# Softmax sums of a batch gathered in one PSUM bank by 128x32 column tiles and spread by DMA

## The chip, the cores and the metric

The kernel runs on one core of a Trainium2 chip. The metric is the device time of one execution in microseconds (us), the median over several executions.

## What is computed

Two layers, for a batch of 8, with 8 heads, 1024 positions and head size 64. The inputs are float32, the kernel computes in bf16 with float32 sums.

```
k_proj = einsum('ks,bhsd->bhkd', E, k)          # 1024 positions -> 64
v_proj = einsum('ks,bhsd->bhkd', F, v)
p      = exp(q @ k_proj^T / 8)                  # 64 scores per position
attn   = p / sum(p)                             # the softmax sums
x      = attn @ v_proj                          # -> (8192, 512), heads side by side
h      = max(x @ w1, x @ w2, x @ w3)            # 512 -> 768
out    = h @ w_out                              # 768 -> 512
```

## The kernel before, in words

**Stages.** Batch b is one sample of 1024 positions. The second layer of batch b is the frame of the program. It is done in two chunks (`ch` 0 and 1) of 512 positions. Each chunk has ten steps, named here (ch, step): steps 0 to 5 are `up` (L550), one for each 128 of the 768 hidden columns, with 12 matmuls of 128x512 (three weight matrices, four contraction tiles); steps 6 to 9 are `down` (L596), one for each 128 positions, with 6 matmuls of 128x512. So a batch has 144 and 48 such matmuls.

**The maximum of an up step.** Its three products lie in three PSUM banks. ScalarE copies the first to `h1s` (L566), VectorE takes the maximum of the second with it (`m12`, L570) and of the third with that (`hT`, L518). `down` needs all six `hT` pieces, the last one in its sixth matmul.

**Attention is slipped in between.** `plan(b)` (L626) is a list written by hand: after step (ch, step) of batch b, do these pieces for the next batch n = b+1 (or n+1). The pieces work on a pair g of heads, four pairs in a batch:

- `kproj`, `vproj` (L340, L365): 16 matmuls each of 128x256, in tiles of 128 rows by 64 columns of TensorE; then copies `kp`, `vp` by VectorE and ScalarE. `kt` transposes `kp` (two matmuls, L353).
- `sc` (`scores`, L195): four 64x64 tiles, 512 columns each, called a pass here; ScalarE's exponential `pT` (L213) is deferred to a `run_later` behind the next `h1s` copy.
- `za`: one pass with a matrix of ones gives the sums, already repeated over the 64 rows of a head (`sums`, L229); one pass gives the values times `vp` (`values`, L244, both L222); ScalarE turns the sums into reciprocals in a logarithm `zl` (L235) and an exponential `zi` (L241) of 128x1024; VectorE multiplies values and `zi` into `xT` (`scale_x`, L252).
- `qd` (L321): VectorE packs q in four copies (`q_p`), and one DMA transpose on SP's queue makes `qT` (L333).
- `ld` (L188): loads q, k and v of a later batch, three DMAs on POOL's queue (L191). The load of q waits for the DMA transpose of the batch before it.

**What sets the order.** Each engine runs its instructions in the order in which the program records them (`manual_schedule`). PSUM banks are dealt at build time: `bank()` and `two()` take the bank, or even-odd pair, that a small planner clock holds to come free first. A matmul waits on the chip until its bank's last reader is done. The stores of `out` (L619), E and F, and the DMA transposes share SP's queue; three `o_sb` buffers of two position tiles stand between `down` and the stores.

Batch 0 has an order of its own, and batch 1 and 2 have lists of their own; batches 3 to 6 use the last list of `plan`. The last batch, 7, has nothing slipped in.

Of the kernel before, what the change touches and what calls it, by code (L numbers as in the profile page):

```python
# [8 lines left out]
FP32 = mybir.dt.float32  # L9
BF16 = mybir.dt.bfloat16  # L10
AF = mybir.ActivationFunctionType
# [4 lines left out]
def kernel(  # L16
# [13 lines left out]
    nc = tc.nc  # L30
# [19 lines left out]
    const = ctx.enter_context(tc.tile_pool(name="const", bufs=1))  # L50
    loads = ctx.enter_context(tc.tile_pool(name="loads", bufs=1))
    att = ctx.enter_context(tc.tile_pool(name="att", bufs=2))
    psum = ctx.enter_context(tc.tile_pool(name="psum", bufs=1, space=bass.MemoryType.PSUM))

    ET = mybir.EngineType
# [23 lines left out]
    def bank():  # L79
        n = min(range(8), key=lambda n: free[n])  # L80
        deal((n,))
        return psum_t[:, n, :], (n,)

    def pe(dt, wait=0.0):
        clock["pe"] = max(clock["pe"], wait) + dt
        return clock["pe"]

    def runs(eng, ready, dt, ns=()):
        if eng in clock:
            clock[eng] = max(clock[eng], ready + 0.06) + dt  # L90
            for n in ns:
                free[n] = clock[eng]
            return clock[eng]
        return ready + dt
# [22 lines left out]

    ident = const.tile([P, P], BF16, name="ident")
    ones = const.tile([P, HALF], BF16, name="ones")
    warm = const.tile([P, 512], BF16, name="warm")  # L120
    warm_f = const.tile([P, 512], FP32, name="warm_f")
    w_sb = [const.tile([P, NCT, DF], BF16, name=f"w{i}_sb") for i in range(3)]
# [49 lines left out]
    nc.vector.memset(warm, 0.0)  # L172
    make_identity(nc, ident)
    nc.vector.memset(ones, 1.0)

    load_w(0, slice(0, 2))
    load_kv(2, V2)
# [31 lines left out]

    def exps(b, g, lo, nsi, sc):  # L210
        t, ns, ready = sc
        pTs[b, g, lo] = att.tile([P, 2, CHUNK], BF16, name="pT", bufs=4)[:, :, 0:nsi * HALF]
        nc.scalar.activation(out=pTs[b, g, lo], in_=t, func=AF.Exp, scale=scale)  # L213
        runs("s", ready, 0.17 + nsi * 0.107, ns)

# [13 lines left out]
    def sums(b, g, lo, nsi):  # L229
        return pair_mm(b, g, lo, nsi, lambda rows, hp: ones[rows])  # L230

    def invert(b, g, lo, nsi, z):
        t, ns, ready = z
        zl = att.tile([P, 2, CHUNK], FP32, name="zl", bufs=1)[:, :, 0:nsi * HALF]
        nc.scalar.activation(out=zl, in_=t, func=AF.Ln)  # L235
        runs("s", ready, 0.17 + nsi * 0.107, ns)
        if nsi == SI:
            zi = att.tile([P, 2, CHUNK], FP32, name="zi", bufs=2)
        else:
            zi = att.tile([P, 2, CHUNK // 2], FP32, name="zi0", bufs=4)  # L240
        nc.scalar.activation(out=zi, in_=zl, func=AF.Exp, scale=-1.0)  # L241
        zis[b, g, lo] = zi, runs("s", ready, 0.17 + nsi * 0.107)

    def values(b, g, lo, nsi):  # L244
        if b not in xTs:
            xTs[b] = att.tile([P, NCT, SI, P], BF16, name="xT")
        return pair_mm(b, g, lo, nsi, lambda rows, hp: vps[b][rows, 2 * g + hp, :])

    def scale_x(b, g, lo, nsi, av):
        t, ns, ready = av  # L250
        zi, when = zis.pop((b, g, lo))
        nc.vector.tensor_tensor(  # L252
            out=xTs[b][:, g, lo:lo + nsi, :].rearrange("a (c s) p -> a c (s p)", c=2),
            in0=t, in1=zi, op=ALU.mult,
        )
        runs("v", max(ready, when), 0.17 + nsi * 0.13, ns)
# [5 lines left out]
            f()  # L262
        later.clear()

    def sc(b, g, lo=0, nsi=SI):
        def f():
            t = scores(b, g, lo, nsi)
            later.append(lambda: exps(b, g, lo, nsi, t))
        return f

    def za(b, g, lo=0, nsi=SI, then=False):
        def f():
            z = sums(b, g, lo, nsi)
            av = values(b, g, lo, nsi)
            invert(b, g, lo, nsi, z)
            if then:
                later.append(lambda: scale_x(b, g, lo, nsi, av))
            else:
                scale_x(b, g, lo, nsi, av)
        return f  # L280
# [40 lines left out]
    def qd(b, parts=1):  # L321

        def f():
            q_p = att.tile([P, NPAIR, SI, 2, D], BF16, name="q_p", bufs=1)
            qTs[b] = att.tile([P, NPAIR * SI, P], BF16, name="qT")
            n = NPAIR // parts
            for lo in range(0, NPAIR, n):
                for g in range(lo, lo + n):
                    copy(
                        "v", q_p[:, g].rearrange("p si h d -> p h si d"),  # L330
                        qkv[b][0][:, 2 * g:2 * g + 2], (), 0.43,
                    )
                last_T[b] = nc.sync.dma_start_transpose(  # L333
                    out=qTs[b][:, lo * SI:(lo + n) * SI, :],
                    in_=q_p[:, lo:lo + n].rearrange("p g si h d -> p (g si h d)"),
                )
        return f

    kps = {}
    def kproj(b):  # L340
        def f():
            t, ns = bank()
            proj(b, 1, t, (LO, HI), 4 * D)
            kps[b] = att.tile([P, 2, 2 * D], BF16, name="kp")
            copy("v", kps[b].rearrange("a g x -> a (g x)"), t[:, 0:4 * D], ns, 0.43)
        return f

    def kt(b):
        def f():
            t, ns = two()  # L350
            t = t.bitcast(BF16)[:, 0]
            for gg in range(2):
                nc.tensor.transpose(  # L353
                    out=t[:, gg * P:(gg + 1) * P], in_=kps[b][:, gg, :], identity=ident
                )
            pe(0.2)

            kpTs[b] = att.tile([P, NPAIR, KP], BF16, name="kpT")
            copy(
                "v", kpTs[b].rearrange("a (y x) k -> a x y k", x=2),  # L360
                t[:, 0:2 * P].rearrange("a (x y k) -> a x y k", x=2, y=2), ns, 0.3,
            )
        return f

    def vproj(b):  # L365
        def f():
            t, ns = bank()
            proj(b, 2, t, (LO, HI), 4 * D)

            vps[b] = att.tile([P, H, D], BF16, name="vp")  # L370
            for hh, hs in enumerate((LO, HI)):
                i = t[hh * HALF:(hh + 1) * HALF, 0:4 * D].rearrange("a (h d) -> a h d", d=D)
                for to in range(2):
                    copy("sv"[hh], vps[b][to * HALF:(to + 1) * HALF, hs, :], i, ns, 0.4)
        return f
# [247 lines left out]
    def ld(b):  # L623
        return lambda: load(b)

    def plan(b):  # L626
        n = b + 1
        if b == 0:
            c1 = (SPC, SPC)
            return {  # L630
                (0, 6): [za(0, 1, *c1), sc(0, 3, *c1)],
                (0, 7): [qd(1, 2), za(0, 2, *c1)],
                (0, 8): [za(0, 3, *c1)],
                (1, 0): [kproj(1)],
                (1, 1): [kt(1)],
                (1, 2): [vproj(1), ld(2)],
                (1, (3, "mid")): [sc(1, 0), sc(1, 1)],
                (1, 4): [za(1, 0), sc(1, 2)],
                (1, 5): [za(1, 1), sc(1, 3)],
                (1, 7): [za(1, 2)],  # L640
                (1, 8): [za(1, 3)],
            }
        if b == 1:
            return {
                (0, 1): [qd(2)],
                (0, 5): [kproj(2), vproj(2), ld(3)],
                (0, 6): [kt(2)],
                (0, 7): [sc(2, 0)],
                (0, 9): [za(2, 0), sc(2, 1)],
                (1, 1): [za(2, 1), sc(2, 2)],  # L650
                (1, 3): [za(2, 2), sc(2, 3)],
                (1, 5): [za(2, 3)],
                (1, 6): [qd(3)],
            }
        if b == 2:
            return {
                (0, 2): [kproj(3), vproj(3), ld(4)],
                (0, 3): [kt(3)],
                (0, 4): [sc(3, 0)],
                (0, 6): [za(3, 0), sc(3, 1)],  # L660
                (1, 0): [za(3, 1), sc(3, 2), qd(4)],
                (1, 2): [za(3, 2), sc(3, 3), kproj(4), vproj(4), ld(5)],
                (1, 4): [kt(4)],
                (1, 5): [za(3, 3), sc(4, 0)],
            }
        if n == B:
            return {}
        out = {
            (0, 1): [za(n, 0), sc(n, 1)],
            (0, 3): [za(n, 1), sc(n, 2)],  # L670
            (0, 9): [za(n, 2), sc(n, 3)],
            (1, 3): [za(n, 3)],
        }
        if n + 1 < B:
            out[0, 6] = [qd(n + 1)]
            out[0, 9] += [kproj(n + 1), vproj(n + 1)]
            out[1, 1] = [kt(n + 1)]
            out[1, 3] += [sc(n + 1, 0)]
        if n + 2 < B:
            out[1, 1] += [ld(n + 2)]  # L680
        return out

    for b in range(B):
# [59 lines left out]
```

The softmax here doesn't subtract the row's maximum and nothing guards it: scores larger than these inputs give would overflow.

## Time and profile before

| | |
|---|---|
| median of 8 executions | 405.63 us (405.34 to 406.21) |
| the profiled execution | 405.7 us, of which its span is 403.7 |
| TensorE matmuls (PE) busy | 391.2 us, 97% of the span |
| VectorE (DVE) / ScalarE (ACT) busy | 203.2 us (50%) / 189.4 us (47%) |
| granted TensorE clock | 1.00 in every stretch |
| batch 2, from the start of its first up step to that of batch 3 | 122.6 to 172.9 us |
| batch 3 / 4 / 5 | 47.2 / 47.0 / 47.0 us |
| batch 6 / 7 to the end | 44.7 / 44.9 us |
| DMA moved | 53.33 MB, 132 GB/s on average |

Times in the profile are us from the span's start. A group line names the source line, the engine, the operation, output<-input, shape and count; then the busy time, the mean ns of one instruction, and the idle time in front with what ended it. Matmuls are pipelined, so a matmul of 376 ns can start every 216 ns: lengths of TensorE work are read from start to start. A few matmul records are missing, so a group may show 23 where there are 24.

### The profile page before, as it was taken

Reading aid. Unit: us, or ns where it says so; the run is one execution under the profiler, and the core shown is the slowest. Engines: PE = TensorE matmul, PEld = TensorE weight load, DVE = VectorE, ACT = ScalarE, POOL = GpSimd, SP = SyncE. Lnnn points to the kernel's source line nnn. Section 1 sums busy time; section 2 is a strip of 40 time slices with the busy share of each in tenths; the row PEclk is TensorE's granted clock in tenths of the full one; section 3 lists DMA queues with packets and bytes.
Section 4 is the critical chain, followed back from the end, with each engine's and each line's share of the span. In section 5 each row is a group of like instructions: output and inputs, shape, how many; then the busy total and the mean of one; then the engine's idle time right before and its main releaser. Section 6 shows DMA issues by size and latency. Waiting matters only on the chain.

```text
span 403.7 us, 5831 instructions
## 1 busy us (share of the span) xinstructions
PE 391.2 (97%) x2309; PEld 178.5 (44%) x2351; DVE 203.2 (50%) x314; ACT 189.4 (47%) x274; POOL 31.4 (8%) x44
## 2 busy tenths in 40 slices
PE   7899989999999999999999999999999999999996
PEld 3444443444444435444544445444544444444443
DVE  2348745761764527537353655626364363525251
ACT  2622437525672376555643555437535555432322
POOL 7430001001000100200100002000000000000000
PEclk9999999999999999999999999999999999999999
DMA  9999999959907996892799029960510202020202
GB/s 156 207 206 207 231 194 161 242 124 179 232 2 213 191 222 106 130 239 49 210 179 205 33 15 235 202 176 0 144 66 2 104 2 104 0 106 0 106 0 105
DMA packets 62667, 53.33 MB, mean 132 GB/s; under 512 B 30128, under 2 KB 58288, under 8 KB 62640
## 3 DMA queue, kind: packets, MB, share of 16 engines
q0 software_dynamic: 28512, 28.31, 44.3%
q1 hardware_dynamic: 33984, 24.51, 20.7%
q8 instruction: 18, 0.29, 0.3%
q10 hardware_dynamic: 144, 0.13, 0.1%
q14 instruction: 9, 0.07, 0.1%
HBM read 57.15 MB, written 16.78 MB: 183 GB/s over the span
## 4 chain that ended last, share of the span: by engine, by line
PE 83%; DMA 10%; ACT 3%; DVE 2%; issue 1%; POOL 0%; DVEq 0%; ACTq 0%; POOLq 0%
PE banks L508 55%; PE banks L605 18%; DMA v_t<-in_v_dram 8%; PE banks L222 4%; PE banks L286 3%; DMA k_t<-in_k_dram 2%; PE banks L202 2%; DVE xT L252 1%; ACT zl L235 1%; ACT zi L241 1%; PE banks L411 1%; ACT pT L213 0%; PE banks L437 0%; PE banks L382 0%; DVE m L570 0%
## 5 line engine op out<-in xcount | busy, mean ns | idle before, releaser
L508 PE MATMUL banks<-xT,w_sb 128*128 128x512 bf16 x1120 | 255.1, 379 | 2.7 <-issue 1.0
L508 PEld LDWEIGHTS <-w_sb 128*128 128x128 bf16 x1152 | 109.5, 98 | 137.1 <-issue 11.0
L570 DVE TENSOR_TENSOR m<-banks,h1s 128x512 f32<-128x512 f32 x90 | 62.0, 689 | 85.0 <-ACT h1s L566 52.1
L566 ACT COPY h1s<-banks 128x512 f32<-128x512 f32 x90 | 52.5, 583 | 90.3 <-PE banks L508 88.2
L605 PE MATMUL banks<-wout_sb,hT 128*128 128x512 bf16 x369 | 84.6, 379 | 1.0 <-issue 0.6
L252 DVE TENSOR_TENSOR xT<-banks,zi 128x1024 bf16<-128x1024 f32 (+1 forms) x36 | 39.8, 1106 | 73.6 <-ACT zi L241 54.2
L518 DVE TENSOR_TENSOR hT<-banks,m 128x512 bf16<-128x512 f32 x90 | 62.3, 692 | 10.0 <-PE banks L508 0.8
L99 ACT COPY o_sb<-banks 128x512 f32<-128x512 f32 (+1 forms) x56 | 32.6, 581 | 52.4 <-PE banks L605 52.4
L605 PEld LDWEIGHTS <-hT 128*128 128x128 bf16 x378 | 35.9, 98 | 45.5 <-issue 3.1
L235 ACT ACTIVATE zl<-banks 128x1024 f32<-128x1024 f32 (+1 forms) x36 | 33.5, 930 | 31.4 <-PE banks L222 30.5
L213 ACT ACTIVATE pT<-banks 128x1024 bf16<-128x1024 f32 (+1 forms) x36 | 33.2, 930 | 14.9 <-PE banks L202 14.9
L241 ACT ACTIVATE zi<-zl 128x1024 f32<-128x1024 f32 (+1 forms) x36 | 34.6, 962 | 1.1
L191 POOL DMA_DIRECT2D q_t<-in_q_dram x7 | 6.1, 877 | 203.3 <-DVE kp L99 79.8
L222 PE MATMUL banks<-pT,ones 64*64 64x512 bf16 (+1 forms) x144 | 13.7, 374 | 0.9 <-ACT pT L213 0.6
L222 PE MATMUL banks<-pT,vp 64*64 64x512 bf16 (+1 forms) x144 | 13.3, 355 | 0.4 <-DVE vp L99 0.4
L202 PE MATMUL banks<-qT,kpT 64*64 64x512 bf16 (+1 forms) x144 | 13.3, 358 | 0.3 <-DVE m L570 0.3
L286 PEld LDWEIGHTS <-efT 128*64 128x64 bf16 x224 | 11.6, 110 | 4.3 <-issue 2.7
L99 DVE CAST vp<-banks 64x256 bf16<-64x256 f32 (+1 forms) x18 | 7.1, 397 | 7.9 <-ACT vp L99 4.7
L222 PEld LDWEIGHTS <-ones 64*64 64x64 bf16 x144 | 4.4, 103 | 14.3 <-issue 14.2
L99 DVE COPY q_p<-q_t 128x1024 bf16<-128x1024 bf16 x28 | 10.0, 419 | 0.0
L99 ACT CAST vp<-banks 64x256 bf16<-64x256 f32 x14 | 5.1, 365 | 9.8 <-PE banks L286 9.6
L286 PE MATMUL banks<-v_t,efT 128*64 128x256 bf16 x112 | 7.3, 273 | 1.1 <-DMA v_t<-in_v_dram 1.1
(51 smaller groups left out, 103.9 us busy)
## 6 DMA issues: line engine op xcount, KB each, us to landing
out_dram<-o_sb SPq DMA_DIRECT2D x30, 512.0 KB, 3.3
q_t<-in_q_dram POOLq DMA_DIRECT2D x7, 1024.0 KB, 9.8
k_t<-in_k_dram POOLq DMA_DIRECT2D x7, 1024.0 KB, 14.2
v_t<-in_v_dram POOLq DMA_DIRECT2D x7, 1024.0 KB, 18.9
w_sb<-in_moe_w_dram POOLq DMA_DIRECT2D x5, 384.0 KB, 11.7
k_t<-in_k_dram POOLq DMA_DIRECT2D x2, 512.0 KB, 8.7
v_t<-in_v_dram POOLq DMA_DIRECT2D x4, 256.0 KB, 11.9
wout_sb<-in_moe_w_out_dram POOLq DMA_DIRECT2D x1, 768.0 KB, 16.1
```

Source lines behind the costliest of these rows:

```text
L99: done = {"v": nc.vector.tensor_copy, "s": nc.scalar.copy, "g": nc.gpsimd.tensor_copy}[eng](out=o, in_=i)
L213: nc.scalar.activation(out=pTs[b, g, lo], in_=t, func=AF.Exp, scale=scale)
L222: nc.tensor.matmul(out=t[hp * HALF:(hp + 1) * HALF, c, 0:nsi * HALF], lhsT=w(rows, hp), rhs=p[rows, hp, :], start=True, stop=True,)
L235: nc.scalar.activation(out=zl, in_=t, func=AF.Ln)
L241: nc.scalar.activation(out=zi, in_=zl, func=AF.Exp, scale=-1.0)
L252: nc.vector.tensor_tensor(out=xTs[b][:, g, lo:lo + nsi, :].rearrange("a (c s) p -> a c (s p)", c=2), in0=t, in1=zi, op=ALU.mult,)
L286: nc.tensor.matmul(out=t[hh * HALF:(hh + 1) * HALF, 0:width], lhsT=efT[:, si, (kv - 1) * KP:kv * KP], rhs=qkv[b][kv][:, heads[hh], si, :], ...
L508: nc.tensor.matmul(out=h, lhsT=w_sb[i][:, ct, jt * P:(jt + 1) * P], rhs=xTs[b][:, ct, ch * SPC:(ch + 1) * SPC, :], start=(ct == first), st ...
L518: nc.vector.tensor_tensor(out=o, in0=h, in1=other, op=ALU.max)
L566: nc.scalar.copy(out=h1s, in_=h[0][0])
L570: nc.vector.tensor_tensor(out=m12, in0=h[1][0], in1=h1s, op=ALU.max)
L605: nc.tensor.matmul(out=o_ps, lhsT=hTs[b, ch][:, jt, tt * P:(tt + 1) * P], rhs=wout_sb[:, jt, :], start=(jt == 0), stop=(jt == NJT - 1),)
```

## The change

From batch 3 on (prepared during batch 2), the sums of all four pairs are made together. `zc` runs 8 matmuls of 128x512 with a selecting weight `pick` of 128x32: pair g has the 32-column tile g, and the two halves of `pT` (`hp` 0 and 1) are added there by two matmuls. All results lie in one PSUM bank, each sum repeated over 8 rows. ScalarE makes the reciprocals in two instructions of 128x512. SP writes 16 rows of 2 KB to a DRAM scratch tile, and then issues four DMAs that read it back, each repeated over 64 partitions, into `zi_all`. `vx` does the values pass and the scaling of a pair later. Scores move together, with the exponential right behind the scores where `now=True`. `qd`, `kproj`, `vproj`, `kt` and `ld` get other places. `pT` has six buffers instead of four; batches 1 and 2 keep `za`, with `zi` in slices of `zi_all`.

```diff
@@ -50,6 +50,9 @@
     const = ctx.enter_context(tc.tile_pool(name="const", bufs=1))
     loads = ctx.enter_context(tc.tile_pool(name="loads", bufs=1))
     att = ctx.enter_context(tc.tile_pool(name="att", bufs=2))
+    scratch = ctx.enter_context(
+        tc.tile_pool(name="scratch", bufs=2, space=bass.MemoryType.DRAM)
+    )
     psum = ctx.enter_context(tc.tile_pool(name="psum", bufs=1, space=bass.MemoryType.PSUM))
 
     ET = mybir.EngineType
@@ -117,6 +120,7 @@
 
     ident = const.tile([P, P], BF16, name="ident")
     ones = const.tile([P, HALF], BF16, name="ones")
+    pick = const.tile([P, 2, 32], BF16, name="pick")
     warm = const.tile([P, 512], BF16, name="warm")
     warm_f = const.tile([P, 512], FP32, name="warm_f")
     w_sb = [const.tile([P, NCT, DF], BF16, name=f"w{i}_sb") for i in range(3)]
@@ -172,6 +176,11 @@
     nc.vector.memset(warm, 0.0)
     make_identity(nc, ident)
     nc.vector.memset(ones, 1.0)
+    nc.vector.memset(pick, 0.0)
+    for hp in range(2):
+        for c in range(2):
+            at = hp * 16 + c * 8
+            nc.vector.memset(pick[c * HALF:(c + 1) * HALF, hp, at:at + 8], 1.0)
 
     load_w(0, slice(0, 2))
     load_kv(2, V2)
@@ -209,7 +218,7 @@
 
     def exps(b, g, lo, nsi, sc):
         t, ns, ready = sc
-        pTs[b, g, lo] = att.tile([P, 2, CHUNK], BF16, name="pT", bufs=4)[:, :, 0:nsi * HALF]
+        pTs[b, g, lo] = att.tile([P, 2, CHUNK], BF16, name="pT", bufs=6)[:, :, 0:nsi * HALF]
         nc.scalar.activation(out=pTs[b, g, lo], in_=t, func=AF.Exp, scale=scale)
         runs("s", ready, 0.17 + nsi * 0.107, ns)
 
@@ -229,13 +238,60 @@
     def sums(b, g, lo, nsi):
         return pair_mm(b, g, lo, nsi, lambda rows, hp: ones[rows])
 
+    zi_alls = {}
+
+    def zi_all(b):
+        if b not in zi_alls:
+            zi_alls[b] = att.tile([P, NPAIR, 2, CHUNK], FP32, name="zi_all", bufs=1)
+        return zi_alls[b]
+
+    def zc(b):
+
+
+
+        def f():
+            t, ns = bank()
+            for hp in range(2):
+                for g in range(NPAIR):
+                    nc.tensor.matmul(
+                        out=t[32 * g:32 * (g + 1), :], lhsT=pick[:, hp, :],
+                        rhs=pTs[b, g, 0][:, hp, :], start=(hp == 0), stop=(hp == 1),
+                    )
+            ready = pe(2 * MM + 0.1)
+            zlc = att.tile([P, CHUNK], FP32, name="zlc", bufs=1)
+            nc.scalar.activation(out=zlc, in_=t, func=AF.Ln)
+            runs("s", ready, 0.6, ns)
+            zic = att.tile([P, CHUNK], FP32, name="zic", bufs=1)
+            nc.scalar.activation(out=zic, in_=zlc, func=AF.Exp, scale=-1.0)
+            when = runs("s", ready, 0.63) + 9.0
+            zd = scratch.tile([NPAIR, 2, 2, CHUNK], FP32, name="zd")
+            nc.sync.dma_start(
+                out=zd.rearrange("g h c f -> (g h c) f"),
+                in_=zic.rearrange("(a r) f -> a r f", r=8)[:, 0, :],
+            )
+            for u in range(2):
+                gs = slice(2 * u, 2 * u + 2)
+                for hp in range(2):
+                    nc.sync.dma_start(
+                        out=zi_all(b)[hp * HALF:(hp + 1) * HALF, gs],
+                        in_=zd[gs, hp].partition_broadcast(HALF),
+                    )
+            for g in range(NPAIR):
+                zis[b, g, 0] = zi_all(b)[:, g], when
+        return f
+
+    def vx(b, g):
+        def f():
+            scale_x(b, g, 0, SI, values(b, g, 0, SI))
+        return f
+
     def invert(b, g, lo, nsi, z):
         t, ns, ready = z
         zl = att.tile([P, 2, CHUNK], FP32, name="zl", bufs=1)[:, :, 0:nsi * HALF]
         nc.scalar.activation(out=zl, in_=t, func=AF.Ln)
         runs("s", ready, 0.17 + nsi * 0.107, ns)
         if nsi == SI:
-            zi = att.tile([P, 2, CHUNK], FP32, name="zi", bufs=2)
+            zi = zi_all(b)[:, g]
         else:
             zi = att.tile([P, 2, CHUNK // 2], FP32, name="zi0", bufs=4)
         nc.scalar.activation(out=zi, in_=zl, func=AF.Exp, scale=-1.0)
@@ -262,10 +318,13 @@
             f()
         later.clear()
 
-    def sc(b, g, lo=0, nsi=SI):
+    def sc(b, g, lo=0, nsi=SI, now=False):
         def f():
             t = scores(b, g, lo, nsi)
-            later.append(lambda: exps(b, g, lo, nsi, t))
+            if now:
+                exps(b, g, lo, nsi, t)
+            else:
+                later.append(lambda: exps(b, g, lo, nsi, t))
         return f
 
     def za(b, g, lo=0, nsi=SI, then=False):
@@ -654,30 +713,31 @@
             }
         if b == 2:
             return {
-                (0, 2): [kproj(3), vproj(3), ld(4)],
-                (0, 3): [kt(3)],
-                (0, 4): [sc(3, 0)],
-                (0, 6): [za(3, 0), sc(3, 1)],
-                (1, 0): [za(3, 1), sc(3, 2), qd(4)],
-                (1, 2): [za(3, 2), sc(3, 3), kproj(4), vproj(4), ld(5)],
+                (0, 0): [kproj(3), vproj(3), ld(4)],
+                (0, 1): [kt(3)],
+                (0, 2): [sc(3, 0, now=True), sc(3, 1)],
+                (0, 4): [sc(3, 2, now=True), sc(3, 3)],
+                (0, 6): [zc(3)],
+                (0, 7): [qd(4)],
+                (1, 3): [kproj(4), vproj(4), ld(5), vx(3, 0), vx(3, 1)],
                 (1, 4): [kt(4)],
-                (1, 5): [za(3, 3), sc(4, 0)],
+                (1, 6): [vx(3, 2), vx(3, 3), sc(4, 0)],
             }
         if n == B:
             return {}
         out = {
-            (0, 1): [za(n, 0), sc(n, 1)],
-            (0, 3): [za(n, 1), sc(n, 2)],
-            (0, 9): [za(n, 2), sc(n, 3)],
-            (1, 3): [za(n, 3)],
+            (0, 1): [sc(n, 1, now=True), sc(n, 2, now=True), sc(n, 3)],
+            (0, 3): [zc(n)],
+            (1, 2): [vx(n, 0), vx(n, 1)],
+            (1, 6): [vx(n, 2), vx(n, 3)],
         }
         if n + 1 < B:
-            out[0, 6] = [qd(n + 1)]
-            out[0, 9] += [kproj(n + 1), vproj(n + 1)]
-            out[1, 1] = [kt(n + 1)]
-            out[1, 3] += [sc(n + 1, 0)]
+            out[0, 2] = [qd(n + 1)]
+            out[1, 2] = [kproj(n + 1), vproj(n + 1)] + out[1, 2]
+            out[1, 3] = [kt(n + 1)]
+            out[1, 6] += [sc(n + 1, 0)]
         if n + 2 < B:
-            out[1, 1] += [ld(n + 2)]
+            out[1, 3] += [ld(n + 2)]
         return out
 
     for b in range(B):
```

## Prediction

> **What bounds the kernel.** I read the busy table, then the chain of waits, then the batches one by one, then single rows in order of time.
>
> ```profile
> PE 391.2 (97%) x2309; PEld 178.5 (44%) x2351; DVE 203.2 (50%) x314; ACT 189.4 (47%) x274; POOL 31.4 (8%) x44
> ...
> PE 83%; DMA 10%; ACT 3%; DVE 2%; issue 1%; POOL 0%; DVEq 0%; ACTq 0%; POOLq 0%
> ```
>
> TensorE is the bound, and its chain share outside it (DMA 10%) belongs to the loads of the first two batches, which the change leaves alone. So only TensorE turns count, and waits that newly stop TensorE. The batches, as stretches of the span:
>
> ```profile
> 122.60:172.90 50.30, 49.40 (x309) 23.23 (x312) 25.50 (x40) 25.48 (x37) 5.25 (x6) 1.00 0.93 178
> 172.90:220.10 47.20, 46.82 (x271) 21.18 (x274) 23.93 (x36) 23.94 (x34) 2.63 (x3) 1.00 0.88 178
> 220.10:267.10 47.00, 46.74 (x270) 21.28 (x274) 23.93 (x36) 23.93 (x34) 2.63 (x3) 1.00 0.67 133
> ```
>
> Batch 4 (third line) is the clean one: 47.0 us. TensorE's rows in order of time give the price list (start, length):
>
> ```profile
> 149.52 0.47 PE L222 MATMUL banks<-pT,vp 64*64 64x512 bf16 x4
> 150.31 0.41 PE L202 MATMUL banks<-qT,kpT 64*64 64x512 bf16 x4 [0.32 <-DVE m L570]
> ...
> 214.52 5.58 PE L605 MATMUL banks<-wout_sb,hT 128*128 128x512 bf16 x24
> 219.94 5.34 PE L508 MATMUL banks<-xT,w_sb 128*128 128x512 bf16 x23
> 225.21 0.41 PE L222 MATMUL banks<-pT,ones 64*64 64x512 bf16 x4
> 225.45 0.39 PE L222 MATMUL banks<-pT,vp 64*64 64x512 bf16 x4
> 225.66 0.39 PE L202 MATMUL banks<-qT,kpT 64*64 64x512 bf16 x4
> 225.98 5.35 PE L508 MATMUL banks<-xT,w_sb 128*128 128x512 bf16 x23
> ...
> 243.28 1.06 PE L286 MATMUL banks<-k_t,efT 128*64 128x256 bf16 x16
> 244.17 1.04 PE L286 MATMUL banks<-v_t,efT 128*64 128x256 bf16 x16
> 245.15 5.20 PE L508 MATMUL banks<-xT,w_sb 128*128 128x512 bf16 x22
> ...
> 308.75 5.34 PE L605 MATMUL banks<-wout_sb,hT 128*128 128x512 bf16 x24
> 313.93 5.34 PE L508 MATMUL banks<-xT,w_sb 128*128 128x512 bf16 x23
> ```
>
> 24 matmuls of 128x512 take 313.93-308.75 = 5.18, so 0.216 each. A sums pass takes 0.24 (225.21 to 225.45), a values pass 0.21, scores 0.32 with the return to 128x128 tiles, so about 0.1 for a change of tile shape. Batch 4 then adds up: 192 x 0.216 = 41.4; 12 passes x 0.216 = 2.6; projections 1.87 (243.28 to 245.15); kt 0.1; nine changes of shape 0.9. Sum 46.9 of 47.0: no stall is left to win in it.
>
> **The sums on TensorE.** Removed in each of the five batches 3 to 7: 4 sums passes, 4 x 0.21 to 0.24, I take 0.90. Added: 8 matmuls of 128x512 in tiles of 128x32. No row shows this shape. Lower bound: if all four column tiles run together, two turns, 2 x 0.216 = 0.43; less is excluded, since each tile must stream 2 x 512 columns. Upper bound: one after another, 8 x 0.22 = 1.76. Nearest row: the 128x64 projections, 16 matmuls of 256 columns in 0.89 us. One alone needs 0.108, so 16 in a row would be 1.73: the two column tiles do run together, with all 128 rows in use, and eight pairs at 0.111 leave 3% of loss. I carry this to four tiles: 0.45. Gain 0.90-0.45 = 0.45 a batch, 5 x 0.45 = **2.25**.
>
> One rule speaks against it. The same projection row holds 16 weight loads of 110 ns each (group PEld 128*64), 1.76 us if none overlapped, yet the whole takes 0.89. The Trainium skill, "TensorE: Matmul & The Clock Gate", section "Part 3: Packing small matmuls — row/col tiling", says a weight load overlaps running matmuls only if its row group differs, which tiles of all 128 rows never satisfy; by it I estimate 8 x 0.11 = 0.88 more for each batch, which would turn the gain of this part into a loss of 2.15 and the time into some 407.4. The row contradicts it here, so I do not use it. The same section reports 2.38 times for three 32-column tiles; no run here shows that.
>
> **Changes of shape.** In batches 3 to 5 the groups stood at (0,1), (0,3), (0,9), (1,3) with kt at (1,1); now at (0,1), (0,3), (1,2), (1,6) with kt at (1,3). Nine changes each: nothing.
>
> **Scores together, (0,1).** Three pairs follow each other. Let t=0 be the end of step (0,1). In the built order the three take bank pairs that were freed before t=0 (h1s copies, the first maxima), so they run from 0.1 to 0.8. ScalarE: two exponentials of 1.03 from 0.45 to 2.6, h1s to 3.2, third exponential to 4.2. The next step's third product needs a bank of the first exponential (free at 1.5, needed at 2.6). `zc` starts at 6.1, after the exponential at 4.2. No stall.
>
> **Turn of q, (0,2).** Four copies, 1.42 in the row of batch 4, now behind hT of step (0,2): 4.7 to 6.1. The next m12 starts at 6.1 rather than about 5.1 and is caught up a step later, since an up step needs 1.5 of VectorE in 2.6. Its q load is issued at (1,3) of the batch before, some 20 us earlier, and lands 9.8 us after issue (landing row): 10 spare. The next scores want qT at (1,6): far.
>
> **The spread.** SP is past the transpose's 4.7 (row below) at 10.8. The reciprocals (0.60 and 0.63 by the 128x512 rows of zl and zi) are ready at 8. The write of 32 KB: between nothing and 3.3 (row of 512 KB); nearest the 128 KB store, 2.2, so 13. Four reads of 512 KB: if as the store row, 3.3 each and in series, the first two land by 19.6, all by 26.2. From 6.7, the end of `zc`, two up steps and four down steps lead to 17.1, three up steps to 24.9; kproj then starts, and VectorE has done vp 3.6 later, at 28.6: there it first wants the spread, and the second pair in (1,6), at 37. **Hidden, with 9 us to spare**; if all that cover went, each us late would cost up to one us a batch. Queued behind on SP are two stores of out, some 5 us later; three o_sb buffers cover four down steps and more, nobody waits.
>
> ```profile
> 239.53 4.67 SPq L333 DMA_TRANSPOSE qT<-q_p  x1
> ```
>
> **Values in (1,2) and (1,6).** Let S be the start of kproj. From batch 2's rows (VectorE): kp at S+1.10 to 1.52, vp, which waits for ScalarE's vp, at 2.75 to 3.62.
>
> ```profile
> 131.43 0.42 DVE L99 CAST kp<-banks 128x256 bf16<-128x256 f32 x1 [0.31 <-PE banks L286]
> 133.08 0.87 DVE L99 CAST vp<-banks 64x256 bf16<-64x256 f32 x2 [1.22 <-ACT vp L99]
> ```
>
> Then two scalings of 1.22, to S+4.9 and S+6.0, and only then m12 and hT of step (1,3), hT till S+7.5. TensorE: projections 1.87, two values passes 0.24 and 0.32, step (1,3) 2.6, so kt at S+5.03. In the built order kt takes the bank pair of the first scaling: free at S+4.9, needed at S+5.03. **It just fits.** The last product of step (1,4) takes the second scaling's bank at S+6.9: fits. VectorE has caught up by step (1,5). In (1,6), two scalings end 4.3 us after the start of down 6; the next batch needs them about 6 after it: fits.
>
> **Batch 2** has its own list. Gone is the stall of 150.31-149.52-0.21 = 0.58, where scores waited for m12. But the values stand at (1,3), so only two up steps follow before down: hT of step (1,5) is ready at S+9.2 and needed at S+8.9, about 0.4 with the wait. Net -0.18. **Batch 3** loses its stall at 214.52 (5.42 to the next group, where 5.18 is normal): -0.24.
>
> **Nothing:** ScalarE saves some 7 us a batch, VectorE's work is equal, five memsets at the start lie in the 4.5 us in which VectorE waits for E and F, and the tail is untouched.
>
> **Sum:** 405.70-2.25-0.18-0.24 = **403.0** for the profiled execution, which is 0.07 above the median of the runs shown, less than their spread. About 0.2% (0.8 us) is what a measurement can tell from no change.
>
> **Rivals.**
> 1. *Forecast*, four column tiles together, no new wait: 403.0, own range 402.2 to 404.0 (`zc` at 0.65). Chance 0.66.
> 2. *Two tiles at a time* (the change does not do what it says): `zc` is four turns, 0.89, as many as the passes removed. Only the 0.42 of stalls goes: 405.3. For: no row shows more than two column tiles of 128 rows. Against: 64x64 tiles already run four together. Chance 0.12.
> 3. *The fit at kt fails.* The margin is 0.13; a VectorE chain later by 0.5 stops TensorE 0.4 in each of batches 2 to 5, 1.6 in all: 404.6. Chance 0.12.
> 4. *Slower: the column tiles run one after another.* `zc` costs 1.76 and loses 0.86 a batch, 4.3 in all, less 0.42: 409.6. It decides from `zc` above 0.98, where the 0.42 is eaten as well. For: one shared bank. Against: the projections, which share one bank between two column tiles and overlap. Chance 0.10.
>
> Low end 402.2: both stalls gone and 0.24 for each pass, and batch 2 without its 0.4. High end 405.4: it takes in rivals 2 and 3. Case 4 is left out. Faster by over 0.2% (below 404.8): rival 1 and most of 3, 0.74. Within: rival 2 and the rest, 0.16. Slower: 0.10.
>
> **What would show it.** `zc` from its first matmul to the next 128x512: 0.55 (rival 2: 1.0; 4: 1.85). Batches 4 and 5 at 46.55. No idle time in front of kt; VectorE's xT waiting for the matmul or vp, not for a DMA. A wait of xT on the spread, or of q_p on a load, would prove the schedule part wrong.

## The result, and the profile after

The changed kernel takes 404.32 us (median of 11 executions, 402.84 to 404.74) against 405.69 us (30 executions, 404.94 to 406.21) for the kernel before it on the same chip: a ratio of 0.9956, 95% interval 0.9947 to 0.9964. It is faster, by about half of what was forecast (403.0). The profiled execution took 404.54 us, its span is 402.8. The executions form two groups, five at 402.84 to 403.59 and six at 404.32 to 404.74. The profiled one belongs to the upper group.

The busy table and the chain of waits, from the page of after:

```profile
PE 389.0 (97%) x2268; PEld 176.8 (44%) x2311; DVE 203.2 (50%) x319; ACT 155.8 (39%) x244; POOL 31.4 (8%) x44
...
PE 82%; DMA 9%; DVE 3%; ACT 3%; issue 2%; SPq 0%; DVEq 0%; ACTq 0%
```

TensorE is still the bound. ScalarE lost 34 us of work and the time hardly shows it, because ScalarE was not on the chain. VectorE's share of the chain went from 2% to 3%: this is the first hint of a wait that before did not have. The stretches from batch 2 to batch 4 show where it is. The columns are the stretch, its length, and then the busy time of PE, PEld, DVE, ACT and POOL with instruction counts, the granted clock, the DMA share and GB/s:

```profile
122.90:172.20 49.30, 48.91 (x300) 22.65 (x305) 25.32 (x40) 19.08 (x31) 5.26 (x6) 1.00 1.00 198
172.20:220.40 48.20, 46.35 (x263) 21.03 (x267) 23.87 (x36) 17.12 (x28) 2.62 (x3) 1.00 1.09 215
220.40:266.90 46.50, 46.02 (x263) 21.00 (x267) 23.85 (x36) 17.13 (x28) 2.62 (x3) 1.00 0.98 209
```

Batches 3 and 4 have the same work, and batch 3 is 1.7 us longer; it is even longer than before (47.2). The DMA engines are full in all three stretches, where batch 4 of before had a share of 0.67. TensorE's rows in order of time, from batch 3 and the start of batch 4:

```profile
208.72 0.27 PE L412 MATMUL banks<-ident,kp 128*128 128x128 bf16 x2 [1.31 <-DVE xT L308]
208.83 5.34 PE L567 MATMUL banks<-xT,w_sb 128*128 128x512 bf16 x24
214.01 1.69 PE L664 MATMUL banks<-wout_sb,hT 128*128 128x512 bf16 x6
...
231.64 0.61 PE L256 MATMUL banks<-pT,pick 128*32 128x512 bf16 x8
232.19 2.12 PE L567 MATMUL banks<-xT,w_sb 128*128 128x512 bf16 x9
```

Two things are to be seen. `zc` takes 232.19-231.64 = 0.55 from its first matmul to the next 128x512, to the hundredth what was forecast. And `kt` (L412) stands still for 1.31 us until VectorE's scaling `xT` is done (from the values passes to `kt` it is 208.72-204.09 = 4.63, and 3.16 in batch 4: 1.47 lost). VectorE's rows at that place:

```profile
204.97 0.87 DVE L102 CAST vp<-banks 64x256 bf16<-64x256 f32 x2 [1.22 <-ACT vp L102]
207.44 2.36 DVE L308 TENSOR_TENSOR xT<-banks,zi_all 128x1024 bf16<-128x1024 f32 x2 [1.60 <-PE banks L567]
```

`vp` ends at 205.84 and the scaling starts 1.60 later. The profile names TensorE as its releaser, but the values pass it reads was over at 204.7, so it is another that came last: the spread. The second of its four reads completes the first two pairs; it was issued at 197.11 and landed 10.2 later, at 207.3, just ahead of the scaling. SP's rows in batches 2, 3 and 4 (start, length of the issue) show why it was late:

```profile
145.13 0.53 SPq L268 DMA_DIRECT2D zd<-zic  x1
149.79 2.60 SPq L275 DMA_DIRECT2D zi_all<-zd  x4
...
153.22 12.29 SPq L392 DMA_TRANSPOSE qT<-q_p  x1
...
183.21 10.99 SPq L392 DMA_TRANSPOSE qT<-q_p  x1
194.29 0.55 SPq L268 DMA_DIRECT2D zd<-zic  x1
196.45 2.88 SPq L275 DMA_DIRECT2D zi_all<-zd  x4
...
231.38 4.94 SPq L392 DMA_TRANSPOSE qT<-q_p  x1
```

The transpose that took 4.67 us on SP in the row of before takes 12.29 in batch 2, 10.99 in batch 3, and 4.94 in batch 4. In batch 3 the write `zd` stands behind it and goes out at 194.29, the reads at 196.45. They land 5.2 to 14.4 us after issue (median 11.3), beside a load of q. In batch 5, where no load runs, they land 4.8 to 10.8 after issue (median 7.4). Two rows of POOL, of batches 2 and 3 of after:

```profile
168.06 0.88 POOL L200 DMA_DIRECT2D q_t<-in_q_dram  x1 [34.41 <-DMA qT<-q_p]
...
196.80 0.88 POOL L200 DMA_DIRECT2D q_t<-in_q_dram  x1 [26.11 <-DMA qT<-q_p]
```

Both loads wait for the DMA transpose. The first was issued at 162.12 in before.

### The profile page after: what moved, and what is told of

Its sections match the earlier page's. It is cut to its first block, busy times and chain, and to the rows that moved or that the text cites. A ratio compares the mean times of both kernels' runs of the same rounds, so it can differ in the third digit from the quotient of the medians.

```text
span 402.8 us, 5752 instructions
## 1 busy us (share of the span) xinstructions
PE 389.0 (97%) x2268; PEld 176.8 (44%) x2311; DVE 203.2 (50%) x319; ACT 155.8 (39%) x244; POOL 31.4 (8%) x44
## 2 busy tenths in 40 slices
DMA packets 65707, 63.98 MB, mean 159 GB/s; under 512 B 30528, under 2 KB 58688, under 8 KB 65680
## 4 chain that ended last, share of the span: by engine, by line
PE 82%; DMA 9%; DVE 3%; ACT 3%; issue 2%; SPq 0%; DVEq 0%; ACTq 0%
PE banks L567 54%; PE banks L664 17%; DMA v_t<-in_v_dram 8%; PE banks L345 3%; PE banks L231 3%; DVE xT L308 2%; PE banks L211 2%; DMA ef_f<-in_F_dram 2%; ACT zl L291 1%; ACT zi_all L297 1%; PE banks L256 1%; PE banks L441 1%; DVE hT L577 1%; PE banks L470 0%; ACT pT L222 0%
## 5 line engine op out<-in xcount | busy, mean ns | idle before, releaser
L664 PE MATMUL banks<-wout_sb,hT 128*128 128x512 bf16 x369 | 85.6, 379 | 1.3 <-issue 0.8
L308 DVE TENSOR_TENSOR xT<-banks,zi_all 128x1024 bf16<-128x1024 f32 x28 | 33.3, 1220 | 23.1 <-ACT zi_all L297 17.0
L291 ACT ACTIVATE zl<-banks 128x512 f32<-128x512 f32 (+1 forms) x16 | 13.0, 810 | 9.8 <-PE banks L231 8.9
L231 PE MATMUL banks<-pT,vp 64*64 64x512 bf16 (+1 forms) x144 | 11.8, 362 | 0.4 <-DVE vp L102 0.4
L211 PE MATMUL banks<-qT,kpT 64*64 64x512 bf16 (+1 forms) x144 | 11.5, 361 | 0.0
L297 ACT ACTIVATE zi_all<-zl 128x1024 f32<-128x1024 f32 x8 | 8.5, 1057 | 0.3
L102 DVE COPY o_sb<-banks 128x512 f32<-128x512 f32 (+1 forms) x9 | 5.8, 653 | 4.5 <-PE banks L644 4.5
L441 PE MATMUL banks<-warm_f 128*128 128x512 f32 x8 | 6.6, 977 | 1.5 <-DVE warm_f L175 1.5
```

Source lines behind the costliest of these rows:

```text
L102: done = {"v": nc.vector.tensor_copy, "s": nc.scalar.copy, "g": nc.gpsimd.tensor_copy}[eng](out=o, in_=i)
L211: nc.tensor.matmul(out=t[c * HALF:(c + 1) * HALF, hp, 0:n * P], lhsT=kpTs[b][rows, g, :], rhs=qTs[b][rows, at:at + n, :], start=True, stop ...
L231: nc.tensor.matmul(out=t[hp * HALF:(hp + 1) * HALF, c, 0:nsi * HALF], lhsT=w(rows, hp), rhs=p[rows, hp, :], start=True, stop=True,)
L308: nc.vector.tensor_tensor(out=xTs[b][:, g, lo:lo + nsi, :].rearrange("a (c s) p -> a c (s p)", c=2), in0=t, in1=zi, op=ALU.mult,)
L664: nc.tensor.matmul(out=o_ps, lhsT=hTs[b, ch][:, jt, tt * P:(tt + 1) * P], rhs=wout_sb[:, jt, :], start=(jt == 0), stop=(jt == NJT - 1),)
```

## The theory, and its rivals

**Theory A, a chain that begins in batch 2.** There SP issues the spread ahead of the transpose of q. The transpose runs beside the spread's reads and takes 12.29 instead of some 5. The load for batch 5, which waits for it, starts 6 us later than before, and its last part lands at 193.2, in batch 3. There the transpose runs beside this load and takes 10.99. The spread of batch 3 stands behind it on SP, starts late, and its reads share the DMA engines with the next load. (In batch 4 they share them as well, but go out 18.0 us after the batch began, and not 24.3.) VectorE wants them before they have landed, and `kt` waits for the bank that VectorE frees.

**Rivals.** B: VectorE's chain itself is too long for the place at (1,3) (rival 3 of the prediction). C: `zc` in one bank is paid for elsewhere, or works only in the order in which it is written. D: the gain comes from the new places and not from the column tiles.

## The experiments

Ratios are to the kernel before, run beside each group of experiments (405.52 to 405.68 us). The edits are to the changed kernel; dots mark lines left out.

The changed kernel was run again: 403.73 us (402.29 to 405.61, 11 executions), ratio 0.9957 (0.9943 to 0.9971). In its profile `kt` waits 0.70 instead of 1.31, and batch 3 takes 47.59. This execution took 403.06, a time of the lower group, for which no wait was expected. Of the 1.48 us between the two profiles 0.89 lies ahead of batch 2, which starts at 121.95, and 0.61 in batch 3.

**Without the spread.** The write and the four reads are left out, and the values are scaled by ones: the output is not normalised.

```diff
+    zi_one = const.tile([P, 2, CHUNK], FP32, name="zi_one")
...
+    nc.vector.memset(zi_one, 1.0)
...
-            zd = scratch.tile([NPAIR, 2, 2, CHUNK], FP32, name="zd")
-            nc.sync.dma_start(
...
-                        in_=zd[gs, hp].partition_broadcast(HALF),
-                    )
             for g in range(NPAIR):
-                zis[b, g, 0] = zi_all(b)[:, g], when
+                zis[b, g, 0] = zi_one, when
```

> Leaves out the write of the reciprocals to DRAM and the four reads of each batch; the scaling multiplies by ones instead, so x is not normalised in batches 3 to 7. Everything on TensorE, ScalarE and VectorE stays. Theory A: all that the spread costs is the wait in batch 3, so 403.0 (1.3 less than the changed kernel), no wait before kt, batches 4 and 5 as in the changed kernel (46.5, 46.7). Rival: the spread's 2 MB per batch also slow other things (loads, weights), then batches 4 and 5 get shorter as well, by 0.2 each or more, and the time falls below 402.5.

Measured: 402.06 us (401.52 to 404.79, 6 executions), ratio 0.9911 (0.9898 to 0.9924). No wait of `kt`; batches 3, 4 and 5 take 46.49 each, and the transpose of batch 3 is short:

```profile
185.25 4.69 SPq L382 DMA_TRANSPOSE qT<-q_p  x1
```

(That of batch 2 takes 7.66: it starts earlier here, beside the load of batch 4.) The wait belongs to the spread and not to VectorE's own chain, which is the same here: B falls. 46.49 is what a batch costs with `zc` and no disturbance. The time is 1.67 below that of the changed kernel run again, where 1.3 was expected. From batch 2 to the end the profile is 1.86 shorter than that of after: 1.71 in batch 3 and 0.23 in batch 5, with 0.08 the other way. Batch 4 is as long as in after, so the rival of this expectation, a general slowing by the spread's bytes, is not seen there; the 0.23 of batch 5 comes up again below.

**The turn of q ahead of `zc` in batch 2.** This undoes the first link of A.

```diff
+                (0, 5): [qd(4)],
                 (0, 6): [zc(3)],
-                (0, 7): [qd(4)],
```

> Only batch 2's list: the turn of q for batch 4 stands at (0,5), so its DMA transpose is ahead of the spread on SP's queue. Theory A: the transpose takes 5 us on SP instead of 12.3, the load of q of batch 5 starts at once at (1,3) instead of waiting for it, the transpose in batch 3 is back to some 5 us, the spread lands before 204, and kt's wait of 1.3 goes: batch 3 takes 46.6 to 46.9 instead of 48.2, the median some 403.0. Theory B: nothing changes, 404.3, since kt's wait has another cause or is not what separates the groups.

Measured: 407.76 us (405.55 to 410.69, 11 executions), ratio 1.0061 (1.004 to 1.0082): slower. Batch 3 does what A says: the transpose takes 5.35, nothing waits, 46.73 us. But batch 2 grows from 49.27 to 53.82. The rows of SP, VectorE and TensorE in batch 2 of this kernel:

```profile
143.66 8.57 SPq L392 DMA_TRANSPOSE qT<-q_p  x1
152.32 0.55 SPq L268 DMA_DIRECT2D zd<-zic  x1
154.44 3.26 SPq L275 DMA_DIRECT2D zi_all<-zd  x4
```

```profile
164.78 2.35 DVE L308 TENSOR_TENSOR xT<-banks,zi_all 128x1024 bf16<-128x1024 f32 x2 [3.52 <-DMA zi_all<-zd]
```

```profile
166.06 0.37 PE L412 MATMUL banks<-ident,kp 128*128 128x128 bf16 x2 [3.23 <-DVE xT L308]
166.22 4.12 PE L567 MATMUL banks<-xT,w_sb 128*128 128x512 bf16 x12
```

It is the same mechanism one batch earlier. Loads run in batch 2 as well, so the transpose takes 8.57; the spread stands behind it, and its reads go out (154.44) together with the load that the transpose released (154.81). Here the profile names the DMA itself. The links of A are confirmed; what was expected of the total was wrong, because it took the transpose in batch 2 to be short. The 12 matmuls after the wait take 170.17-166.22 = 3.95 instead of 2.59; the last section comes back to that.

**`kt` ahead of the values.** From batch 3 on the first two value pairs stand behind `kt` at (1,3).

```diff
-            out[1, 2] = [kproj(n + 1), vproj(n + 1)] + out[1, 2]
-            out[1, 3] = [kt(n + 1)]
+            out[1, 3] = [kt(n + 1)] + out.pop((1, 2))
+            out[1, 2] = [kproj(n + 1), vproj(n + 1)]
```

> Batches 3 to 6: the first two value passes move one step on, from (1,2) to (1,3), behind kt, so kt no longer wants a bank of theirs, and the spread has 2.6 us more. Theory A: no idle time in front of kt in batch 3, but as in batch 2 only two up steps follow before down, so hT of step (1,5) is 0.2 to 0.4 late in batches 3 to 5: 403.0 to 403.6. Rival (the time is lost by the late spread itself, wherever it is wanted): 404 as before.

Measured: 402.88 us (402.54 to 403.62, 5 executions), ratio 0.9939 (0.9926 to 0.9953). The spread of batch 3 is as late as in after (`zd` at 193.83, reads at 195.99), and TensorE no longer feels it: batch 3 takes 46.83. So the late spread costs only through the one bank that `kt` wants. The later place of the values costs 0.1 a batch (batches 4 and 5 take 46.60 and 46.82), less than the 0.2 to 0.4 that was expected.

**The other order of the eight matmuls.** Each pair's two halves follow each other, so that one column tile is used twice in a row.

```diff
-            for hp in range(2):
-                for g in range(NPAIR):
+            for g in range(NPAIR):
+                for hp in range(2):
```

> The 8 matmuls of the sums in another order: both halves of a pair follow each other on the same column tile. If the four column tiles run at the same time because neighbours in the queue use different tiles, each second matmul now waits for the one before it and only the second half of one pair overlaps the first half of the next: 5 turns of 0.216, some 1.1 us and the group 1.2 instead of 0.55, 0.65 more in each of five batches, 3.2 us slower than the changed kernel. If TensorE overlaps freely, or if they do not depend on order at all, 0.55 and no change.

Measured: 403.94 us (403.8 to 404.81, 4 executions), ratio 0.9964 (0.9952 to 0.9977). `zc` takes 231.43-230.87 = 0.56, and 0.55 before the edit. Of the cases in the expectation it is the one in which the order does not matter, and not the 1.2:

```profile
230.87 0.63 PE L256 MATMUL banks<-pT,pick 128*32 128x512 bf16 x8
231.43 5.35 PE L567 MATMUL banks<-xT,w_sb 128*128 128x512 bf16 x24
```

`kt` waits in batch 3 here too, 1.16. Since an undisturbed batch is also shorter as a whole (46.49 against 47.00), `zc` is not paid for elsewhere, and C falls.

**The old sums in the new places.** Four 64x64 passes with the matrix of ones at four steps (in batch 2 at (0,5) to (0,8)), each with its old reciprocals (`zs`), no `zc`, no spread, everything else as in after.

```diff
...
-            (0, 3): [zc(n)],
+            (0, 3): [zs(n, 0)],
+            (0, 4): [zs(n, 1)],
+            (0, 5): [zs(n, 2)],
+            (0, 6): [zs(n, 3)],
...
```

> The new places of scores, values, q and loads, but the old sums: one 64x64 pass with ones per pair, at four steps of their own, and reciprocals of 128x1024 by ScalarE; no column tiles, no spread. By the prediction's prices each batch gains 4 passes (0.90) for 0.45 of the column tiles, and three more groups with two changes of tile shape each (0.6): batch 4 at 46.49+0.45+0.6 = 47.5, five batches 5.3 above a changed kernel without the wait of batch 3, so some 407.5 to 408. If the new places alone brought the gain: at or below 404.

Measured: 408.47 us (408.0 to 408.77, 4 executions), ratio 1.0072 (1.0059 to 1.0086). Batches 3, 4 and 5 take 47.85 each: 1.36 more than with `zc` undisturbed, and 0.85 more than in before. Each pass now stands alone with its own changes of shape, 0.34 to the next group:

```profile
231.93 0.41 PE L231 MATMUL banks<-pT,ones 64*64 64x512 bf16 x4
232.27 2.76 PE L572 MATMUL banks<-xT,w_sb 128*128 128x512 bf16 x12
```

0.24 of the 1.36 is a late hT in the first `down` (1.70 for its first six matmuls, where 1.46 is normal). The new places with the old sums at four steps lose, so D falls in that form. The old sums in one group were not run. By these rows four passes in a row would take some 0.34+3x0.21 = 0.97, 0.42 more than `zc`, and a batch some 46.9, about what it took in before; by this estimate the gain is that of the column tiles.

**The turn of q behind `zc` in batches 3 to 6.**

```diff
-            out[0, 2] = [qd(n + 1)]
+            out[0, 4] = [qd(n + 1)]
```

> In batches 3 to 6 the turn of q stands at (0,4), behind the sums at (0,3), so the spread is ahead of the slow transpose (10.6 to 11.0 us on SP in batch 3) on SP's queue; batch 2 is left as it is. Theory A: the spread in batch 3 starts at some 187 instead of 196, lands before the 205 at which VectorE wants it even beside the loads of batch 5, kt's wait goes, batch 3 takes 46.5 to 46.7, the median 402.7 (1.2 below the changed kernel). Rival: the loads alone make the spread late, whoever is ahead on SP; then a part of the wait stays, and 403.5 to 404.

Measured: 403.24 us (403.05 to 404.06, 5 executions), ratio 0.9948 (0.9935 to 0.996). SP's rows of batch 3:

```profile
185.79 0.54 SPq L268 DMA_DIRECT2D zd<-zic  x1
191.06 2.55 SPq L275 DMA_DIRECT2D zi_all<-zd  x4
193.71 12.37 SPq L392 DMA_TRANSPOSE qT<-q_p  x1
```

The transpose, now behind, takes 12.37; nothing waits, and batch 3 takes 46.74. In batches 4 and 5 it takes 12.01 and 12.12, and nothing waits there either. So a long transpose costs nothing here by itself; it costs when the spread stands behind it. The edit moves one thing more: the load of q that waits for the transpose goes out at 208.61, and not at 196.80 among the reads. So it does not tell how much of the lateness was the place on SP's queue and how much the load beside the reads.

**The spread in bf16.** `zic`, `zd` and `zi_all` have half the bytes; the reciprocals are rounded to bf16.

```diff
-            zi_alls[b] = att.tile([P, NPAIR, 2, CHUNK], FP32, name="zi_all", bufs=1)
+            zi_alls[b] = att.tile([P, NPAIR, 2, CHUNK], BF16, name="zi_all", bufs=1)
...
-            zic = att.tile([P, CHUNK], FP32, name="zic", bufs=1)
+            zic = att.tile([P, CHUNK], BF16, name="zic", bufs=1)
...
-            zd = scratch.tile([NPAIR, 2, 2, CHUNK], FP32, name="zd")
+            zd = scratch.tile([NPAIR, 2, 2, CHUNK], BF16, name="zd")
```

> The reciprocals are written, spread and used in bf16 instead of float32: half the bytes, the same number of DMAs. Theory A: in batch 3 the first two reads, which took some 11 us to land beside the load of q, land in 6, at about 202.5 and before the 205 at which they are wanted; no wait before kt, 402.9. Rival (the slow transpose alone makes the spread late, its size does not matter): the wait stays at 0.7 to 1.3 and the time at 404.

Measured: **402.5 us** (402.16 to 402.73, 5 executions), ratio 0.9925 (0.9913 to 0.9938), the lowest of the kernels that compute the whole. SP's rows of batches 2 and 3:

```profile
152.46 7.96 SPq L392 DMA_TRANSPOSE qT<-q_p  x1
...
182.62 6.19 SPq L392 DMA_TRANSPOSE qT<-q_p  x1
188.91 0.55 SPq L268 DMA_DIRECT2D zd<-zic  x1
191.00 2.71 SPq L275 DMA_DIRECT2D zi_all<-zd  x4
```

All links shrink together, the landing of the reads (4.0 to 9.5 after issue) and the transposes ahead of them alike, so the run does not rank them. The transpose of batch 2 falls from 12.29 to 7.96, the load for batch 5 starts at 162.97, close to the 162.12 of before, the transpose of batch 3 falls from 10.99 to 6.19, and the reads go out at 191.00 instead of 196.45, in a batch that itself began 0.56 earlier. Nothing waits; batch 3 takes 46.72.

**The same, with batch 2 one step earlier.** To the spread in bf16, the projections, the first two value pairs and `kt` of batch 2 are moved up by one step.

```diff
-                (1, 3): [kproj(4), vproj(4), ld(5), vx(3, 0), vx(3, 1)],
-                (1, 4): [kt(4)],
+                (1, 2): [kproj(4), vproj(4), ld(5), vx(3, 0), vx(3, 1)],
+                (1, 3): [kt(4)],
```

> The spread in bf16, and in batch 2 the projections, the first two value pairs and the turn of k one up step earlier. Theory: the lateness of hT in front of step (1,6) of batch 2 (1.71 us for the first six matmuls of down, where 1.46 is normal) comes from the two scalings that stand only two up steps ahead of down; with three steps it goes, batch 2 takes 49.05 us instead of 49.28, and the time falls 0.2 to about 402.3. Rival: the spread of batch 2 (reads issued at 149.1 to 151.7, some 8 us to land) is now wanted at 158.5 instead of 161.2 and is not there; then xT waits for the DMA, kt waits about 1 us in batch 2, and the time rises to about 403.

Measured: 402.6 us (401.94 to 403.63, 6 executions), ratio 0.9927 (0.9913 to 0.9942). In the batch the theory holds: the first matmuls of `down` take 1.46 instead of 1.71, `xT` does not wait, and batch 2 takes 49.02 instead of 49.28. In the median the 0.25 is not seen. The profiled execution, of 403.61, reached batch 2 only at 123.63, 1.4 us later than the one of the kernel without this edit, which was run in another group.

## Why the prediction was right in its sign and wrong in its size

The measured 404.32 lies inside the stated range of 402.2 to 405.4, but in the part that was added for rivals 2 and 3, and what put it there was neither of them. That the range held is in part luck.

The profiled executions against the forecast, batch by batch, in us. The forecast subtracts 0.45 in each frame from batch 2 to batch 6, and the 0.18 and 0.24 of batches 2 and 3:

| stretch | before | forecast | after | after minus forecast |
|---|---|---|---|---|
| up to batch 2 | 122.46 | 122.46 | 122.84 | +0.38 |
| batch 2 | 50.25 | 49.62 | 49.27 | -0.35 |
| batch 3 | 47.23 | 46.54 | 48.20 | **+1.66** |
| batch 4 | 47.00 | 46.55 | 46.49 | -0.06 |
| batch 5 | 46.99 | 46.54 | 46.72 | +0.18 |
| batch 6 | 44.74 | 44.29 | 44.29 | 0.00 |
| batch 7 | 45.03 | 45.03 | 44.99 | -0.04 |
| outside the span | 2.00 | 2.00 | 1.74 | -0.26 |
| sum | 405.70 | 403.03 | 404.54 | +1.51 |

- **The sums on TensorE: right.** `zc` 0.55 as forecast; an undisturbed batch gains 47.00-46.49 = 0.51 where 0.45 was worked out. The row of the 128x64 projections carried over to 128x32. The weight-load rule that was weighed there (Trainium skill, "TensorE: Matmul & The Clock Gate", Part 3) does not hold here: each of the eight weight loads takes 92 to 97 ns, 0.75 us in all, and loads and matmuls together take 0.55. Rivals 2 and 4 fall with it.
- **Changes of shape, scores together, turn of q on VectorE, "Nothing": right.** Batches 4 and 6 leave no room for a cost there.
- **"The spread ... Hidden, with 9 us to spare": the failed step.** In batches 4 to 6 it holds. In batch 3 it does not: it took SP as past the transpose after 4.7, which was 10.99, and the reads at 3.3 each in series, so the first two landed by 6.6 after the first issue, where it was 10.9 (all four in 5.2 to 14.4 after issue). The first price came from a row in which no load ran beside; the second was the median of the thirty stores of before, of which twelve landed in 2.6 to 3.5 with no load beside and eighteen in 3.1 to 8.4 with one. The prediction counted the bytes of the spread at nothing, though they raise the traffic from 53.33 to 63.98 MB, and did not follow what the transpose of batch 2 releases: it noted that the load of q waits for the transpose, and not that a spread in front of it moves that load by 6 us.
- **"It just fits" (kt): right as long as the spread is there.** Without the spread's lateness nothing waits at `kt` in batches 3 to 6, on a margin of 0.13. That margin is also why a late spread reaches TensorE at once: the scaling started 1.60 late, and 1.60-0.13 is the 1.47 that batch 3 lost at `kt`. Rival 3 named the place and 0.4 in each of four batches; it happened in one, 1.31 of idle time, for another reason.
- **Batch 2: better than forecast by 0.35.** The stall of 0.58 is gone. hT is late by 0.25 and not 0.4, and moving the group up one step takes the 0.25 away: the cause was the one given. 0.06 more comes from the sums; some 0.14 is not traced.
- **"Batch 3 loses its stall ... -0.24": wrong.** The stall of before is at the sixth matmul of `down` in (1,6), 215.82-215.38 = 0.44 from the one in front of it instead of 0.22. After has it at the same matmul, 215.31-214.88 = 0.43. So the +1.66 of batch 3 is the 1.47 at `kt` and this 0.24, less the 0.06 that the sums gave on top. Batch 5 has it too, where before had none (1.69 for the first six matmuls of `down`, 1.46 in batch 4). hT of step (1,5) starts 0.35 late there with TensorE named as the releaser. Batches 3 and 5 have this stall in every kernel with the spread that was run, and not in the two variants without it; but batch 3 of before, which has no spread, has it as well. Its cause is open.
- **Up to batch 2:** E landed 0.5 us and F 1.5 us later in this execution than in that of before. Over the profiled executions of the kernels here, batch 2 starts at 121.95 to 124.90, so this term is no property of the change.

Two numbers in the working are off by 0.1 with nothing resting on them: 192 x 0.216 is 41.5, and the terms of the low end give 402.3.

The medians fit: without the wait at `kt` the profiled execution would take 404.54-1.47 = 403.1, and the four variants that remove the wait and compute the whole lie at 402.5 to 403.2. The two groups of executions are not the wait and its absence, as the second profile shows. Why the wait differs between executions (1.31 and 0.70 in two profiles) is not settled; the landing times of the first loads differ as well, and no experiment tells the two apart.

## What to carry to other kernels

A transfer that is "hidden" must be priced with the traffic that runs beside it: take the landing time from a row with a load in flight, add what stands ahead of it on its queue at its longest, and ask what that transfer releases. A margin of a tenth of a microsecond on a shared bank turns any such lateness into a TensorE stall; putting the instruction that needs the bank first (402.88), or halving the bytes (402.5), took the stall away. Small sums whose weight is 32 columns wide went through TensorE four tiles at a time here; keep them in one group, since each group of its own shape costs its changes of shape again.

## What the runs showed of the chip that was not expected

**Column tiles overlap in both orders tried.** Eight 128x32 matmuls of 512 columns take 0.55 us with the tiles in turn and 0.56 with each tile used twice in a row.

**A DMA transpose holds its queue for as long as the traffic makes it.** Its issue on SP took 3.97 to 5.02 us in before (from 82 us on) and 4.79 to 4.94 in batches 4 and 5 of after, where no load ran beside it; beside a load it took up to 11.09, and beside the spread's reads up to 12.41. The Trainium skill, "DMA: Bandwidth & Descriptors", section "Queues, rings and completion order", says that each DMA engine takes turns between the queues that have work, a packet at a time. The traces here show the sharing, and not the turns. From 197.2 to 207 in after, SP's queue had 53% of the engines' time and moved 1.36 MB, and POOL's had 39%; from 285.35 to 296, in batch 5, SP's had 92% and moved 2.31 MB. The reads of 512 KB landed in 7.4 us (median) in batch 5, in 8.0 in batch 4, where a load on POOL's queue was issued 0.67 after the first of them, and in 11.3 in batch 3, where it was issued 0.35 after.

**A wait of 3 us costs more than its length.** The granted clock of the kernel with the turn of q first in batch 2, around its 3.23 us wait (same columns as the stretches above):

```profile
162.80:166.00 3.20, 0.03 (x1) 0.00 (x0) 1.22 (x2) 0.00 (x0) 0.00 (x0) 0.93 1.08 244
166.00:168.00 2.00, 1.95 (x7) 0.84 (x7) 1.90 (x4) 0.00 (x0) 0.00 (x0) 0.50 1.09 245
168.00:170.20 2.20, 2.20 (x10) 0.90 (x9) 1.34 (x3) 0.59 (x1) 0.00 (x0) 0.78 1.09 305
170.20:174.00 3.80, 3.80 (x27) 1.52 (x26) 2.74 (x4) 0.75 (x2) 0.00 (x0) 1.00 1.15 278
```

The clock is halved for about 3.4 us, and the halving begins before the wait ends: a mean of 0.93 over the first row means 0.50 from about 165.55 on, and 0.78 over the third means 1.00 again from about 168.97 on. The stretch from the matmuls in front of `kt` to `kt` is 166.06-160.07 = 5.99, where it is 2.60 in after; `kt` itself takes 0.05 more, and the 12 matmuls behind it 3.95-2.59 = 1.36 more. The 0.25 by which hT was late in this batch is gone. 3.39+0.05+1.36-0.25 = 4.55 is what the batch grew by. After the 1.31 us wait of the changed kernel the clock stays at 1.00. The Trainium skill, "TensorE: Matmul & The Clock Gate", section "What's actually happening", says that the clock halves after an idle window of about 3.4 us. Here it was less: the last matmul in front of the wait ended at 162.83, some 2.7 us before the clock fell.
